# Attention scores of two batches from float32r halves of keys and queries

## Chip, cores and metric

One core of a Trainium2 chip. The metric is the device time of one execution in microseconds (us); a change of 0.5% is about 3.1 us here.

## The reference, cut to what matters

```python
scores = scale * np.matmul(q, k.transpose(0, 1, 3, 2))   # B, H, S, D = 4, 8, 768, 64
scores = np.where(keep, scores + bias, -1e9)             # 8 global keys, 96 local ones
a = softmax(scores)                                      # along the keys
x = np.matmul(a, v)                                      # per head, laid out as (B, S, H * D)
h = np.maximum(x.T @ w_tok1, 0.0) @ w_tok2               # mixes along the sequence
u = x + h.T
out = u + np.maximum(u @ w_ch1, 0.0) @ w_ch2             # mixes along the channels
```

Everything is float32 at the interface; the weights arrive as 64-bit floats.

## The kernel before

Attention goes in 48 units called pairs, numbered v = 0 to 47, twelve to a batch. A pair is two heads (n counts the four pairs of heads) and one strip of 256 queries (j = 0, 1, 2). A strip needs few keys, so its scores are two cuts of 128 queries each: for j = 0 the first cut has 128 keys and the second 256, for j = 1 and 2 both have 256. `load` (L335) brings one tile of 128 rows, which holds keys (columns 0 to 383), queries (384 to 639) and values; rows 0 to 63 belong to the first head, rows 64 to 127 to the second. From batch 1 on these tiles are a ring of four, and a load waits for the values step V of four pairs before.

Each pair then runs through named steps: q (`scale`, L347: the queries times a factor; on GpSimd from batch 1 on, into a tile `qs` of a pool of two buffers), S (`scores`, L374: per cut one unsplit float32 product for each head, the two heads in the two halves of the rows of TensorE), max and exp, sum, inverse and norm, a transpose (through TensorE in early pairs, by DMA from pair 20 on, with `split`, `turn` and `join`), V (`values`, L455, two heads in halves of the columns) and put. The keys are read from the loaded tile `e`, the results go to `sp` in PSUM.

After its twelve pairs a batch goes through `tokens` (L515): transposes N (`xtp`), products J (`pj`) and U (`pu`), which leave u as two float32r parts `uh` and `ul`. Then `channel` (L604) runs 24 rounds k of twelve products F (into `hp`), a ReLU split into `hh` on ScalarE and `hl` on VectorE, and twelve products G (into `acc`). These products are already made of three float32r ones: high by high, high by low, low by high. F of a batch needs u of that batch, and S of a batch from 2 on waits for the last `ul` of the batch before (L486). So scores of batch 2 run among F and G of batch 1, and those of batch 3 among those of batch 2.

The order on every engine comes from a planner (`Plan.record`, L109): a list scheduler with costs in us written beside each step, a rank for each, tokens for buffers (`room`, L240; the one token "q" is held from q to the end of S), and a penalty for a change of the form of TensorE's products ("rows" for S, "columns" for V, none for the others; L155). `InOrder` (L189) keeps each engine's instructions in the order in which the planner recorded them; what an instruction waits for at run time is its data and buffers. All instructions made through it carry line L197, so the rows are told apart by tile names.

Of the kernel before, what the change touches and what calls it, by code (L numbers as in the profile page):

```python
# [8 lines left out]
F32 = mybir.dt.float32  # L9
F32R = mybir.dt.float32r  # L10
# [5 lines left out]
ALU = mybir.AluOpType  # L16
# [4 lines left out]
B, H, S, D = 4, 8, 768, 64  # L21
# [3 lines left out]
P = 128  # L25
NS = S // P
NU = NS // 2
NF = FF // P
# [3 lines left out]
AHEAD = 5  # L32
WIDE = 15
RING = 4
FAR = 20
WARM = 2
PER = H // 2 * NU
# [7 lines left out]
def f32(ap):  # L45
    return ap.bitcast(F32)


class Early:


    def __init__(self, tc, pool, pk, nb):
        nc = tc.nc

        self.slots = [pool.tile([P, 1024], F32, tag=f"e{i}", name=f"e{i}") for i in range(3)]
        self.ni = pool.tile([P, 4], I32, tag="ni", name="ni")
        self.ident = pool.tile([P, P], F32, tag="ident", name="ident")
        self.sc = pool.tile([P, H // 2], F32, tag="sc", name="sc")

        def load(out, in_):  # L60
            tc.stamp_issue_order_token(nc.sync.dma_start(out=out, in_=in_).ins, "loads")

        t = self.slots[2]
        self.warm = t[:, 576:832].bitcast(BF16)
        nc.vector.memset(self.warm, 0.0)
        load(self.slots[0][:, 128:640], pk[0, :, 128:640])
        load(self.ni, nb.broadcast_to([P, 4]))
        load(self.slots[0][:, 640:896], pk[0, :, 640:896])
        load(self.slots[1][:, 128:896], pk[1, :, 128:896])

        def iota(t, base, step, mult):
            nc.gpsimd.iota(t, pattern=[[step, t.shape[-1]]], base=base, channel_multiplier=mult,
                           allow_small_or_imprecise_dtypes=True)

        for h in range(H):
            nc.gpsimd.memset(self.sc[64 * (h % 2):64 * (h % 2) + 64, h // 2:h // 2 + 1], float(2 ** (h + 1)))

        self.rel, self.far, self.glob = t[:, 0:224], t[:, 224:448], t[:, 448:576]
        iota(self.rel, 96, -1, 1)
        iota(self.far, -768, 8, -8)  # L80
        nc.gpsimd.affine_select(out=self.far, in_=self.far, compare_op=ALU.is_ge, fill=-BIG, base=96,
                                pattern=[[-1, 224]], channel_multiplier=1)
        iota(self.glob, 0, 1, 0)
        make_identity(nc, self.ident)


class Plan:
# [13 lines left out]
    def add(self, name, engine, cost, run, after=(), rank=0.0, take=(), give=(), form=None):  # L101

        costs = engine if isinstance(engine, dict) else {engine: cost}
        self.work[name] = dict(name=name, costs=costs, run=run, after=sorted(set(after)), rank=rank, take=take, give=give,
                               form=form, choice=isinstance(engine, dict))
# [98 lines left out]
class Fast:  # L206
# [3 lines left out]
    def __init__(self, ctx, tc, early, pk, nb, w1, w2, wc1, wc2, out):  # L210
        self.tc, self.nc = tc, tc.nc
        nc = tc.nc
        self.pe, self.dve, self.act, self.pool, self.sp = [
            InOrder(tc, e) for e in (nc.tensor, nc.vector, nc.scalar, nc.gpsimd, nc.sync)]
        self.pk, self.nb, self.out = pk, nb, out
        self.pieces = [(x, i) for x in (w1, w2) for i in range(0, 2 * S, 512)]
        self.pieces += [(x, C * f) for f in range(NF) for x in (wc1, wc2)]

        def pool(name, bufs, **kw):
            return ctx.enter_context(tc.tile_pool(name=name, bufs=bufs, **kw))  # L220

        const = self.const = pool("const", 1)

        self.ring = early.slots + [const.tile([P, 1024], F32, tag=f"r{i}", name=f"e{i}") for i in range(RING - 3)]
        self.prep = pool("prep", 2)
        self.soft = pool("soft", 8)
        self.mix = pool("mix", 4)
        self.xs = pool("xs", 8)
        self.us = pool("us", 8)
        self.hl = pool("hl", 6)  # L230
        self.io = pool("io", 3)
        self.wt = pool("wt", 2 * NF)
        self.ps = pool("ps", 1, space=PSUM)
        self.early = early
        self.ident, self.sc = early.ident, early.sc
        self.t, self.x, self.u = {}, {}, {}
        self.W1 = [const.tile([P, NS * TOK], F32R, tag=f"w1{x}", name=f"w1{x}") for x in "hl"]
        self.W2 = [const.tile([P, 2 * S], F32R, tag=f"w2{x}", name=f"w2{x}") for x in "hl"]
        self.A, self.Z = {}, {}
        self.plan = Plan(dict(w=2 * NF, raw=AHEAD, t=3, p=6, mix=4, q=1, x=8, u0=8, u1=8, hl=6), BUSY,  # L240
                         dict(dve=self.dve, act=self.act, pool=self.pool))

    def bank(self, name, *key):
# [91 lines left out]
    def load(self, v):  # L335

        b, n, j = where(v)
        if v < 2:
            t = self.early.slots[v]
        else:  # L340
            t = self.wt.tile([P, 1024], F32, tag="w", name="unit") if b == 0 else self.ring[(v - PER) % RING]
            k0, z = (128, 896) if j == 0 else (0, 1024)
            self.sp.dma_start(out=t[:, k0:z], in_=self.pk[v, :, k0:z])
        vs = [[t[:, o:o + 64] for o in (640 + 128 * e, 704 + 128 * e, 896 + 64 * e)] for e in range(2)]
        self.t[v] = dict(k=t[:, 0:384], q=t[:, 384:640], v=vs)

    def scale(self, v, engine):  # L347

        n = where(v)[1]
        if v < 2:  # L350
            self.load(v)
        t = self.t[v]
        t["qs"] = qs = self.prep.tile([P, 256], F32, tag="qs", name="qs")
        sc = self.sc[:, n:n + 1]
        if engine is self.dve:
            engine.tensor_scalar(out=qs, in0=t["q"], scalar1=sc, scalar2=None, op0=ALU.mult)
        elif engine is self.act:
            engine.activation(out=qs, in_=t["q"], func=AF.Copy, scale=sc)
        else:
            engine.tensor_scalar(out=qs, in0=t["q"], scalar1=sc, scalar2=0.0, op0=ALU.mult, op1=ALU.add)  # L360

    def pair(self, v):

        add = self.plan.add
        dve, act, pool = self.dve, self.act, self.pool
        b, n, j = where(v)
        wide = v < WIDE
        far = v >= FAR

        cuts = ((128, 128, 128), (256, 256, 128)) if j == 0 else ((0, 256, 0), (256, 256, 128))  # L370
        c0 = 1 if j == 0 else 0
        g = {}

        def scores():  # L374
            t = self.t[v]
            g["sp"] = [self.bank("sp", v, e) for e in range(2)]
            for i, (o, w, k0) in enumerate(cuts):
                for e in range(2):
                    r = slice(64 * e, 64 * e + 64)
                    self.pe.matmul(out=g["sp"][e][:, o:o + w], lhsT=t["qs"][r, 128 * i:128 * i + 128],  # L380
                                   rhs=t["k"][r, k0:k0 + w], start=True, stop=True)
# [94 lines left out]
        r = rank("pair", v)  # L476
        if v > 1:
            add(f"load{v}", "sp", 1.4 if j == 0 else 1.85, lambda: self.load(v),
                [f"V{v - RING}"] if v >= PER + RING else [f"V{v - PER}"] if v in (PER, PER + 1) else [], rank("load", v),
                ["w"] if v < PER else [])  # L480
        if v:
            add(f"q{v}", dict(dve=0.3, act=0.4, pool=0.56) if b == 0 else dict(pool=0.56), 0, lambda e: self.scale(v, e),
                [f"load{v}"] if v > 1 else [], r - 8, ["q"])
        wp = ["w"] if wide else ["p", "p"]

        add(f"S{v}", "pe", 0.86 if j else 0.65, scores, ([f"q{v}"] if v else []) + ([f"ul{b - 1}7"] if b > 1 else []), r,  # L486
            [("sp", v, 0), ("sp", v, 1)], ["q"], "rows")
        for e in range(2):
            add(f"max{v}{e}", "dve", 0.7 if j else 0.57, lambda e=e: maxima(e), [f"S{v}"] + ([f"max{v}0"] if e else []),
                r - 10, wp if e == 0 else [], [("sp", v, e)])  # L490
# [202 lines left out]
def where(v):  # L693

    b, r = divmod(v, PER)
    j, n = divmod(r, H // 2)
    return b, n, j
# [5 lines left out]
BUSY = dict(dve=1.9, act=1.4, pool=3.6, sp=2.6)  # L703
# [269 lines left out]
```

## Time and profile before

| what | us |
|---|---|
| median of 3 runs | 629.82 |
| lowest and highest | 627.41, 630.03 |
| the profiled execution | 627.44 |
| its span, first to last instruction | 625.9 |

The span is cut into engines: PE is TensorE's products and PEld its weight loads, DVE VectorE, ACT ScalarE, POOL GpSimd. The profiled execution is at the low end of the three runs; about 1.5 us of it lie outside the span.

### The profile page before, as it was taken

The numbers are of one execution on the slowest core, as the hardware profiler recorded it, in microseconds if no ns is written. First come the engines' busy times: TensorE is split into PE (matmuls) and PEld (weight loads), VectorE is DVE, ScalarE is ACT, GpSimd is POOL, SyncE is SP. The second block draws the span as 40 slices with busy tenths as digits, with TensorE's granted clock in tenths as the row PEclk, the third lists the DMA queues.
The fourth block names the chain that finished last, engine by engine and source line by source line (L and its number), as shares of the span: only waits on it lengthen the run. The fifth ranks groups of instructions, "written<-read, shape, count | busy, mean of one in ns | idle before, by whom it ended". The sixth has DMA issues, their size and how long they took to land.

```text
span 625.9 us, 10504 instructions
## 1 busy us (share of the span) xinstructions
PE 607.2 (97%) x3778; PEld 550.7 (88%) x3778; DVE 354.7 (57%) x922; ACT 258.7 (41%) x712; POOL 201.3 (32%) x312
## 2 busy tenths in 40 slices
PE   5899998999999999999999999999999999999995
PEld 3577896998989999888888999889888999999995
DVE  4999999998733215776663337656765335113112
ACT  5899856763423003565563314545442212111110
POOL 4897755662401001544330114344320024000000
PEclk9999998999999999999999999999999999999998
DMA  6960565333540001576663002565433001001001
GB/s 242 404 230 2 202 234 204 129 109 84 119 84 1 2 0 51 96 174 168 144 129 84 0 1 76 126 148 139 137 56 62 0 1 52 1 0 51 1 0 57
DMA packets 71228, 59.49 MB, mean 95 GB/s; under 512 B 56960, under 2 KB 61184, under 8 KB 71168
## 3 DMA queue, kind: packets, MB, share of 16 engines
q1 hardware_dynamic: 71168, 58.74, 33.5%
q8 instruction: 32, 0.52, 0.3%
q14 instruction: 28, 0.23, 0.1%
HBM read 38.80 MB, written 6.29 MB: 72 GB/s over the span
## 4 chain that ended last, share of the span: by engine, by line
PE 83%; DVE 9%; ACT 3%; POOL 2%; issue 1%; DMA 1%; SPq 0%; DVEq 0%; POOLq 0%; ACTq 0%
PE acc L197 30%; PE hp L197 29%; PE sp L197 7%; PE op L197 6%; DVE t L197 5%; PE pj L197 5%; PE pu L197 4%; ACT pp L197 1%; PE xtp L197 1%; PE tp L197 1%; POOL pp L197 1%; DVE p L197 1%; POOL p L197 1%; DMA e<-pk 1%; DVE x L197 1%
## 5 line engine op out<-in xcount | busy, mean ns | idle before, releaser
L197 PE MATMUL hp<-uh,wc 128*128 128x384 f32 x768 | 210.8, 337 | 0.1
L197 PE MATMUL acc<-hh,wc 128*128 128x384 f32 x768 | 199.6, 341 | 0.0
L197 PEld LDWEIGHTS acc<-hh,wc 128*128 128x128 f32 x768 | 137.1, 189 | 8.3 <-issue 6.7
L197 PEld LDWEIGHTS hp<-uh,wc 128*128 128x128 f32 x768 | 139.9, 188 | 3.1 <-issue 0.8
L197 ACT ACTIVATE hh<-hp 128x384 fp32r<-128x384 f32 x96 | 47.1, 490 | 220.5 <-PE hp L197 201.6
L197 DVE SCALAR_TENSOR_TENSOR hl<-hp,hh 128x384 fp32r<-128x384 f32 x96 | 53.1, 553 | 149.0 <-ACT hh L197 149.0
L197 PE MATMUL acc<-hl,wc 128*128 128x384 f32 x384 | 129.0, 336 | 0.2 <-DVE hl L197 0.2
L197 PE MATMUL hp<-ul,wc 128*128 128x384 f32 x384 | 128.5, 335 | 0.0
L197 POOL TENSOR_SCALAR p<-p,st 128x256 f32<-128x256 f32 (+1 forms) x132 | 82.1, 640 | 44.0 <-ACT p L197 19.6
L197 DVE COPY r<-p 128x1024 uint16<-128x1024 uint16 (+1 forms) x94 | 68.1, 737 | 32.7 <-POOL p L197 17.0
L197 POOL TENSOR_TENSOR ul<-x,uh 128x384 fp32r<-128x384 f32 x24 | 24.6, 1027 | 156.2 <-ACT uh L197 90.0
L197 PEld LDWEIGHTS acc<-hl,wc 128*128 128x128 f32 x384 | 72.3, 188 | 0.5 <-DVE hl L197 0.5
L197 PEld LDWEIGHTS hp<-ul,wc 128*128 128x128 f32 x384 | 72.1, 188 | 0.0
L197 ACT ACTIVATE p<-p,st 128x256 f32<-128x256 f32 (+1 forms) x132 | 63.7, 486 | 18.0 <-DVE st L197 10.9
L197 DVE SCALAR_TENSOR_TENSOR t<-w,t 128x512 int32<-128x512 int32 x60 | 51.9, 865 | 1.1
L197 POOL TENSOR_SCALAR qs<-e,sc 128x256 f32<-128x256 f32 x36 | 21.9, 608 | 90.2 <-DMA e<-pk 53.9
L197 PE MATMUL sp<-e,qs 64*128 64x256 f32 (+1 forms) x304 | 42.0, 396 | 3.9 <-ACT x L197 1.5
L197 PEld LDWEIGHTS sp<-e,qs 64*128 64x128 f32 x304 | 26.2, 195 | 13.4 <-issue 6.8
L197 POOL TENSOR_SCALAR pp<-pp,st 128x256 f32<-128x256 f32 (+1 forms) x60 | 34.9, 597 | 8.0 <-DVE st L197 5.7
L197 DVE TENSOR_TENSOR pl<-xtp,ph 128x512 fp32r<-128x512 f32 x24 | 15.5, 686 | 25.6 <-ACT ph L197 25.6
L197 PE MATMUL op<-r,e 128*64 128x128 f32 (+1 forms) x304 | 29.7, 321 | 0.0
L197 POOL TENSOR_TENSOR wc<-t,wc 128x512 fp32r<-128x512 f32 x16 | 22.7, 1419 | 19.5 <-ACT wc L197 18.2
(89 smaller groups left out, 742.1 us busy)
## 6 DMA issues: line engine op xcount, KB each, us to landing
w<-wc SPq DMA_DIRECT2D x24, 512.0 KB, 5.2
e<-pk SPq DMA_DIRECT2D x24, 512.0 KB, 3.6
out<-o SPq DMA_DIRECT2D x32, 192.0 KB, 1.9
e<-pk SPq DMA_DIRECT2D x13, 384.0 KB, 3.7
unit<-pk SPq DMA_DIRECT2D x8, 512.0 KB, 9.0
w<-w SPq DMA_DIRECT2D x6, 512.0 KB, 9.4
p<-r SPq DMA_TRANSPOSE x56, 3.2
unit<-pk SPq DMA_DIRECT2D x2, 384.0 KB, 3.7
```

What stands on the lines that cost most here:

```text
L197: ins = getattr(self.engine, name)(*args, **kw)
```

## The change

For pairs from number 24 on (batches 2 and 3) q now writes its result over the queries in the loaded tile. A new step qh on ScalarE copies keys and queries (640 columns, or 512 for j = 0) to a float32r tile, a new step ql on VectorE or GpSimd, whichever the planner finds free, subtracts that from the original to give the low part. Both parts lie in a pool with one buffer, under a new token "qk" that is held from qh to the end of S; the token "q" is given back after ql. S makes each product as three float32r ones (high by high, high queries by low keys, low queries by high keys), the two heads next to each other in the order, and its planned cost changes.

```diff
+PARTS = 24
+        self.parts = pool("parts", 1)
-        self.plan = Plan(dict(w=2 * NF, raw=AHEAD, t=3, p=6, mix=4, q=1, x=8, u0=8, u1=8, hl=6), BUSY,
+        self.plan = Plan(dict(w=2 * NF, raw=AHEAD, t=3, p=6, mix=4, q=1, qk=1, x=8, u0=8, u1=8, hl=6), BUSY,
-        self.t[v] = dict(k=t[:, 0:384], q=t[:, 384:640], v=vs)
+        self.t[v] = dict(t=t, k=t[:, 0:384], q=t[:, 384:640], v=vs)
-        t["qs"] = qs = self.prep.tile([P, 256], F32, tag="qs", name="qs")
+        qs = t["qs"] = t["q"] if v >= PARTS else self.prep.tile([P, 256], F32, tag="qs", name="qs")
+        def high():
+
+            z = 128 * c0
+            t = self.t[v]["t"][:, z:640]
+            g["qk"] = [self.parts.tile([P, 640], F32R, tag=x, name="qk")[:, z:] for x in "hl"]
+            act.copy(out=g["qk"][0], in_=t)
+
+        def low(engine):
+            h, l = g["qk"]
+            engine.tensor_tensor(out=l, in0=self.t[v]["t"][:, 128 * c0:640], in1=f32(h), op=ALU.subtract)
+
         def scores():
             t = self.t[v]
             g["sp"] = [self.bank("sp", v, e) for e in range(2)]
+            if v >= PARTS:
+                z = 128 * c0
+                for i, (o, w, k0) in enumerate(cuts):
+                    for n, (x, y) in enumerate(((0, 0), (0, 1), (1, 0))):
+                        for e in range(2):
+                            r, q = slice(64 * e, 64 * e + 64), 384 - z + 128 * i
+                            self.pe.matmul(out=g["sp"][e][:, o:o + w], lhsT=g["qk"][x][r, q:q + 128],
+                                           rhs=g["qk"][y][r, k0 - z:k0 - z + w], start=n == 0, stop=n == 2)
+                return
+        ready = f"q{v}"
+        if v >= PARTS:
+            add(f"qh{v}", "act", 0.63 if j else 0.52, high, [f"q{v}"], r - 8, ["qk"])
+            add(f"ql{v}", dict(dve=0.76 if j else 0.62, pool=1.7 if j else 1.35), 0, low, [f"qh{v}"], r - 8, (), ["q"])
+            ready = f"ql{v}"
-        add(f"S{v}", "pe", 0.86 if j else 0.65, scores, ([f"q{v}"] if v else []) + ([f"ul{b - 1}7"] if b > 1 else []), r,
-            [("sp", v, 0), ("sp", v, 1)], ["q"], "rows")
+        add(f"S{v}", "pe", ((0.7 if j else 0.53) if v >= PARTS else 0.86 if j else 0.65), scores, ([ready] if v else []) + ([f"ul{b - 1}7"] if b > 1 else []), r,
+            [("sp", v, 0), ("sp", v, 1)], ["qk"] if v >= PARTS else ["q"], "rows")
```

## Rows read from the trace of the kernel before

**Rows 1.** The page's busy time of each engine, share of the span, instructions.
```profile
PE 607.2 (97%) x3778; PEld 550.7 (88%) x3778; DVE 354.7 (57%) x922; ACT 258.7 (41%) x712; POOL 201.3 (32%) x312
```

**Rows 2.** Busy time by stretch: engines in turn, granted clock, DMA share, GB/s.
```profile
150.00:247.00 97.00, 97.00 (x580) 91.89 (x579) 41.52 (x92) 26.77 (x63) 13.94 (x20) 1.00 0.21 50
247.00:320.00 73.00, 72.96 (x472) 61.96 (x472) 49.18 (x161) 40.28 (x119) 28.41 (x50) 1.00 0.65 140
320.00:382.00 62.00, 62.00 (x370) 58.47 (x368) 27.59 (x54) 20.00 (x45) 12.96 (x17) 1.00 0.19 49
382.00:464.00 82.00, 82.00 (x545) 73.19 (x544) 53.20 (x167) 37.60 (x119) 30.00 (x50) 1.00 0.52 119
464.00:520.00 56.00, 56.00 (x329) 53.08 (x330) 23.66 (x47) 14.30 (x35) 9.85 (x13) 1.00 0.10 20
```

**Rows 3.** The chain that ended last, 235 to 520 us: start, us, what, count.
```profile
by line: PE acc L197 37.9%; PE hp L197 32.3%; PE op L197 8.2%; PE sp L197 8.1%; PE pu L197 5.8%; PE pj L197 5.8%; PE xtp L197 1.8%; issue 0.0%
...
250.94 0.86 PE sp L197 x8
...
264.56 2.08 PE hp L197 x12
...
271.60 2.29 PE hp L197 x12
273.89 1.06 PE sp L197 x8
...
317.44 1.93 PE sp L197 x16
...
336.84 1.75 PE xtp L197 x16
...
339.63 5.49 PE pj L197 x24
...
375.00 6.24 PE hp L197 x36
...
382.28 1.51 PE sp L197 x16
...
498.51 8.32 PE pu L197 x48
```

**Rows 4.** Groups by form, 240 to 480 us: busy us, mean ns, idle before.
```profile
L197 PE MATMUL sp<-e,qs 64*128 64x256 f32 x160 | 22.5, 395 | 0.0
...
L197 POOL TENSOR_SCALAR qs<-e,sc 128x256 f32<-128x256 f32 x22 | 12.7, 579 | 72.7 <-DMA e<-pk 48.0 <-DVE st L197 7.8 <-issue 6.3
...
L197 POOL TENSOR_TENSOR ul<-x,uh 128x384 fp32r<-128x384 f32 x8 | 8.1, 1019 | 46.7 <-ACT uh L197 30.5 <-DVE o L197 16.1
...
L197 ACT CAST uh<-x 128x384 fp32r<-128x384 f32 x10 | 5.1, 513 | 8.4 <-DVE o L197 4.6 <-DVE x L197 3.8
...
L197 PE MATMUL sp<-e,qs 64*128 64x128 f32 x32 | 3.8, 310 | 0.0
...
L197 ACT CAST ph<-xtp 128x512 fp32r<-128x512 f32 x6 | 3.2, 588 | 7.4 <-PE xtp L197 5.5 <-PE pj L197 1.9
...
L197 DVE TENSOR_TENSOR ul<-x,uh 128x384 fp32r<-128x384 f32 x3 | 1.7, 554 | 0.2
```

**Rows 5.** Timeline of the weight loads, 247.5 to 248.3 us (pair 24).
```profile
247.62 0.60 PEld L197 LDWEIGHTS sp<-e,qs 64*128 64x128 f32 x8 [0.25 <-issue]
```

**Rows 6.** Timeline of GpSimd, 262 to 277 us: start, us, [idle before and releaser].
```profile
266.13 0.48 POOL L197 TENSOR_SCALAR qs<-e,sc 128x256 f32<-128x256 f32 x1 [1.31 <-DMA e<-pk]
271.39 0.48 POOL L197 TENSOR_SCALAR qs<-e,sc 128x256 f32<-128x256 f32 x1 [4.78 <-DMA e<-pk]
```

**Rows 7.** Timeline of TensorE, 262 to 277 us (pairs 28 and 29).
```profile
267.38 1.13 PE L197 MATMUL sp<-e,qs 64*128 64x256 f32 x8
...
273.82 1.13 PE L197 MATMUL sp<-e,qs 64*128 64x256 f32 x8
```

**Rows 8.** Busy time of hp's instructions: PE, PEld, DVE, ACT, clock, DMA.
```profile
519.15:626.00 106.85, 53.45 (x288) 50.05 (x288) 13.36 (x24) 11.81 (x24) 0.98 0.07 24
```

## The prediction

> **What bounds the kernel now.** I read the page's busy times first: TensorE has work in 97% of the span, the next engine, VectorE, in 57% [rows 1]. A busy TensorE can still hide waits, so the stretches come next. From 150 to 520 us, which takes in everything that the change touches, TensorE is busy in all but 0.04 us, at full granted clock (1.00, the 2.4 GHz level), while VectorE is busy in 53.2 of 82.0 us in the densest stretch, ScalarE in 37.6 and GpSimd in 30.0 [rows 2]. The chain that ended last says the same: between 235 and 520 us it is products from end to end, 8.1% of them scores, and the time put down to waiting is nil [rows 3]. So here a product that gets shorter brings the end forward by what it gives up, and work on the other engines costs nothing until a product waits for it.
>
> **Products of a pair with 256 keys.** There are 16 such pairs among the 24 (j = 1 and 2). The float32 product is two loads and two passes of products for each head (160 rows of 256 columns and 32 of 128 [rows 4] are 192, eight for each of 24 pairs). Eight in a row for a single pair take 1.06 us on the chain, sixteen for two pairs 1.93 [rows 3]: a further pair costs 0.87 us, four steps of 0.217, since both heads run side by side. In the new form it is six steps of 256 columns. No such product is in the trace, but float32r products of the full array are: 36 of 384 columns take 6.24 us, 0.173 each, and 24 of 512 columns 5.49 us, 0.229 each [rows 3]. The line through both gives 0.117 for 256 columns (0.173 less 0.056). Six steps are 0.70 us, so 0.17 less than 0.87, and 16 pairs give **-2.7 us**. Bounds: a step cannot be below 0.109, the pace of sixteen float32 transposes (1.75 us [rows 3]) that also load 128 columns each time, so -3.4 us; and if the fixed part of a float32r step came on top of the full float32 pace of 0.109 (0.013 more, what 0.173 has above 384 columns at 2.4 GHz), 0.122 a step and -2.2 us.
>
> **Products of a pair with j = 0.** There are 8. Two such pairs take 1.51 us and one 0.86 [rows 3], so one costs 0.65. New: three steps of 256 columns at 0.117, and three of 128. The line would give 0.062 for these, but each brings a load of 128 columns, and the transposes show that a load and a product of this length come no closer than 0.109. I take 0.109: 0.68 in all, 0.03 more than before, **+0.2 us** for 8. Lower bound: the line, -0.9 us. Upper bound: a product of 128 columns in float32r no faster than the unsplit one, which needs two steps of 0.109: +2.9 us. The nearest rows are the loads, so I stay at the 0.109.
>
> What speaks against the change here is a rule of the Trainium skill ("TensorE: Matmul & The Clock Gate", section "LDWEIGHTS (loading the stationary operand)"): a load's time goes by its columns, P / 1.2 ns, and not by its rows, so half the rows save nothing; 128 columns are 107 ns by it, as an estimate. By that the j = 0 pairs come out at no gain, as they do from the transposes, where a count of columns streamed would give 8 x 0.17 = 1.4 us. The trace agrees in the loads' pace (0.109).
>
> **Side by side.** The eight loads of pair 24 all lie within 0.60 us [rows 5]. One after another at 0.109 they would take 0.87, so the two halves load at the same time, and the steps above hold for both heads.
>
> **Changes of form.** Twelve F products take 2.08 us after their like and 2.29 after a score or value step; a score step alone takes 1.06 where its marginal price is 0.87 [rows 3]. So each change of form costs 0.2 us. Before, four score steps stand doubled on the chain (two of each kind; one of each in [rows 3]). With one buffer for the parts, the copy of the next pair begins only when S of this pair is done, and copy plus subtraction take over 1.5 us (next paragraph), so doubles cannot stay without a wait. Taken apart, each costs two more changes, 0.4 us, together 1.6 us; where a value step stands between the two scores it costs nothing. Bounds 0 and +1.6. The order is made anew by the planner; I take **+0.6 us**.
>
> **The split.** Removed: nothing but a buffer; q has the same instruction and place on GpSimd. Added: 24 copies on ScalarE. 384 columns take 513 ns and 512 take 588 [rows 4], so 640 take some 0.66 us; 16 x 0.66 + 8 x 0.59 = 15 us. 24 subtractions: 384 columns take 0.554 us on VectorE and 1.019 on GpSimd [rows 4], by the columns 0.92 or 1.70 for 640 and 0.74 or 1.36 for 512; 21 us on VectorE or 38 on GpSimd. Their cover is the idle time: in 247 to 320 and 382 to 464 us VectorE has 52.6 us free of 155, ScalarE 77.1, GpSimd 96.6 [rows 2]. Without that cover the time is not theirs in full, but what S then waits. Where S waits: q, copy and subtraction are now a chain of 0.66 + 0.92 = 1.6 us (2.4 with GpSimd) longer before it. q itself is often late, as GpSimd spends 48.0 us waiting for loads of `e` [rows 4]. For pair 28 q ends at 266.61 and S starts at 267.38; for pair 29 it is 271.87 and 273.82 [rows 6, 7]. With the longer chain, pair 28 is ready 0.8 to 1.6 us after that place, pair 29 at most 0.5 us after it. The planner knows nearly the same length (0.63 + 0.76) and will put other products ahead, of which F and G give two us at a time; it does not know of queues on ScalarE and VectorE. Behind a copy that waits for S stand exp of an older pair and the ReLU of `hp`, for which the next G waits. Bounds 0 and the whole lateness of these two pairs, 2.1 us; I take **+0.7 us**.
>
> **Attention as a whole** gets later by some 2 us for each turn of the ring, three turns a batch, so about 6 us. Tokens of batch 3 end their products at 506.8 (498.51 + 8.32) [rows 3], but the 288 F products of its channel part start only at 519.15 [rows 8]: 12 us of the work of batch 2 are left to fill in. Nothing.
>
> **Sum.** -2.7 + 0.2 + 0.6 + 0.7 = -1.2 us against the profiled execution's 627.44 (span 625.9 and 1.5 around it), so 626.2. That execution is 2.4 us below the median of the three runs; against the median of 629.82 it is **628.6 us**.
>
> **Rivals.**
> 1. *More of the gain is kept.* Steps at 0.109, no double lost, no wait: -3.4 us and nothing else, 626.4. For it: no product waited between 150 and 520 us before, in spite of chains as long. Against: the float32r rows of 384 and 512 columns stand above a pure stream.
> 2. *S becomes a wait (slower).* The subtraction is late at the place that the planner gave S, as ScalarE's and VectorE's queues are in order. The price: if the four doubled scores stay doubled and each waits 1.6 to 2.4 us, that is 6.4 to 9.6, with pairs 28 and 29 up to 11.7; less the 2.5 of the products, +4 to +9 us, 634 to 639. It decides from waits of 2.5 us in total on, and is slower by over 0.5% from 5.6. Against: 0.04 us of idle TensorE in rows 2.
> 3. *A half's next load is not hidden behind its own product (slower).* Then a step is 0.109 + 0.117 for 256 columns, 0.109 + 0.062 for 128. A pair takes 1.36 instead of 0.87 (16 x 0.49) or 1.19 instead of 0.65 (8 x 0.54): +12 us, 642. Against it: for full rows a load is hidden in the F rows (0.173 a step), and in halves the old step of 0.217 has no room for 0.109 on top of 256 columns in two passes. The Trainium skill has such a rule (same page, "Part 3: Packing small matmuls"): a load overlaps a product in flight only where the row group differs. Rows 3 speak against it.
> 4. *Attention ends too late.* If the longer chain moves the tokens of a batch by more than the 12 us, TensorE idles for the rest: at twice the 6 us, nothing; at three times, +5 net, 635.
>
> **How the numbers follow.** My sum, with its terms within their bounds, has 0.72; rival 1 has 0.12, rival 2 0.09, rival 3 0.04, rival 4 0.03. About 0.5%, 3.1 us, is what a measurement of this kernel can tell from no change. With every term at its bound my sum runs from -3.4 - 0.9 = -4.3 to -2.2 + 2.9 + 1.6 + 2.1 = +4.4 us; the terms are seldom all good or all bad, so its own range is 626 to 631.5. Most of it is within 0.5%; of rival 1 some two thirds are beyond it, with a chance or two from an order that also saves changes of form: faster 0.11. Rivals 2 to 4 and the upper corner of the sum are slower: 0.17. The rest, 0.72, is no difference. The range that leaves out 2 in 10 is 625 to 633.
>
> **What would show it.** After: twelve products a pair in `sp`, the pace of two steps of one head 0.117 for 256 columns and 0.109 for 128; S alone on the chain 0.9 us for either kind; no score steps doubled without an idle TensorE ahead of the second; TensorE busy without gaps from 247 to 480 us; copies of 0.66 us on ScalarE. The prediction is wrong if TensorE shows idle time released by the new subtraction, if the steps are above 0.13, or if 128 columns take 0.2.

## The result and the profile after

The changed kernel takes 631.91 us (median; 630.66 to 634.13) against 629.07 for the kernel before in the same measurement: ratio 1.0052, interval 1.0037 to 1.0066. The time lies in the range that was given, but it is slower where a slight gain was forecast.

The page's busy times of the changed kernel, and its chain that ended last, 240 to 530 us (the view cuts this line off at its end):

```profile
PE 611.0 (97%) x3874; PEld 555.8 (88%) x3874; DVE 370.8 (59%) x929; ACT 269.2 (43%) x732; POOL 235.6 (37%) x333
...
by line: PE acc L198 28.7%; PE hp L198 26.5%; PE pu L198 5.7%; PE op L198 5.7%; PE pj L198 5.7%; PE sp L198 5.3%; DVE r L198 4.9%; POOL p L198 3.2%; DMA p<-r 2.9%; DVE p L198 2.1%; issue 2.1%; PE xtp L198 1.8%; DMA out<-o 1.6%; ACT p L198 1
```

Against [rows 1] GpSimd has 34 us more. The chain is no longer products from end to end, as it was in [rows 3]: the copy `r` on VectorE, GpSimd's norm `p` and DMA are on it.

The profiled execution (633.99 us, span 631.9) is among the slowest of its kernel and the one before was among the fastest, so their spans overstate the difference. What the change can touch is read more exactly from a stretch between two products: from the last G product of batch 0, just ahead of the first G of batch 1, to the first F of batch 3. Timelines of TensorE, the kernel before, then the changed one (start, us):

```profile
240.07 0.34 PE L197 MATMUL acc<-hl,wc 128*128 128x384 f32 x1
...
519.15 0.33 PE L197 MATMUL hp<-uh,wc 128*128 128x384 f32 x1
```

```profile
242.21 0.33 PE L198 MATMUL acc<-hl,wc 128*128 128x384 f32 x1
...
526.27 0.33 PE L198 MATMUL hp<-uh,wc 128*128 128x384 f32 x1
```

The stretch took 279.1 us and takes 284.1: +5.0. (2.1 us of the longer span lie ahead of it, where the granted clock was 0.96 on average between 60 and 150 us, for 0.98 in the kernel before.) I use this stretch for all kernels below, and split it in three: the products of S, the changes of form at 0.2 us each (counted in the order of the trace: 73 before, 81 after), and waits, which are the rest. So "waits" is a remainder against the kernel before, not a sum of waits seen.

The products did what was forecast. Chain of the changed kernel, pieces with scores:

```profile
321.16 0.91 PE sp L198 x12
...
386.88 0.89 PE sp L198 x12
```

A pair with 256 keys in both cuts takes 0.91 for 1.06, a pair with j = 0 0.89 for 0.86 [rows 3]: 16 x -0.15 + 8 x 0.03 = -2.2 us. So 5.0 = -2.3 (as e4 below measures it) + 8 x 0.2 + 5.7 of waits. TensorE's weight loads name who was late (240 to 490 us: total, times, longest):

```profile
PEld op L198 <- DVE r L198: 2.7, 4, 1.4
PEld sp L198 <- DVE hl L198: 1.6, 1, 1.6
PEld op L198 <- DVE st L198: 1.5, 3, 1.0
```

These are mostly value steps `op` that wait for VectorE's copy `r`, and one S that waits for `hl`. No line of this view names the parts `qk`: no product was seen to wait for the subtraction itself. The first of them in the timeline, 260.7 to 264.2 us (GpSimd, VectorE, TensorE):

```profile
260.71 1.28 POOL L198 TENSOR_TENSOR qk<-e,qk 128x512 fp32r<-128x512 f32 x1
260.78 1.64 DVE L198 COPY r<-p 128x768 uint16<-128x768 uint16 x1 [0.29 <-POOL p L198]
...
262.46 0.65 PE L198 MATMUL op<-r,e 128*64 128x256 f32 x2
...
263.44 0.59 DVE L198 COPY r<-p 128x768 uint16<-128x768 uint16 x1
...
264.09 0.43 PE L198 MATMUL op<-r,e 128*64 128x256 f32 x2 [0.98 <-DVE r L198]
```

The copy of 16-bit words, 768 columns wide, takes 0.59 us when alone (263.44). The one that starts 0.07 us after a subtraction on GpSimd takes 1.64: it ends at 262.42, 0.43 after the subtraction (261.99). All that VectorE has behind it is late by 1.0 us, the next such copy among it, and V waits for that one. The planner gave GpSimd 21 of the 23 subtractions between 240 and 490 us, and eleven copies there take over 1.1 us (none did before). The two groups by form, 240 to 490 us:

```profile
L198 POOL TENSOR_TENSOR qk<-e,qk 128x640 fp32r<-128x640 f32 x14 | 22.8, 1628 | 31.7 <-ACT qk L198 31.7
L198 DVE COPY r<-p 128x768 uint16<-128x768 uint16 x27 | 21.6, 810 | 8.0 <-POOL p L198 5.0 <-DMA p<-r 2.9
```

The mean copy of this form took 623 ns in the kernel before, by the same view.

The Trainium skill describes this ("SBUF — State Buffer", section "Who interferes with whom"): VectorE in its two-port modes, which copies can enter, and GpSimd share a pair of ports, whoever comes first has it for its whole instruction, and the other is blocked and not slowed. The trace agrees, in both directions. The twelve copies that start while GpSimd subtracts end 0.42 to 0.47 us after it with 768 columns and 0.55 to 0.70 with 1024, a little less than such a copy takes alone (medians of 0.56 and 0.75). The two subtractions that start 0.10 and 0.18 us into a copy take 2.01 and 1.97 us, the other twelve of 640 columns 1.55 to 1.58:

```profile
439.33 2.01 POOL L198 TENSOR_TENSOR qk<-e,qk 128x640 fp32r<-128x640 f32 x1 [0.36 <-ACT qk L198]
```

### The profile page after: what moved, and what is told of

Its sections match the earlier page's. It is cut to its first block, busy times and chain, and to the rows that moved or that the text cites. A ratio compares the mean times of both kernels' runs of the same rounds, so it can differ in the third digit from the quotient of the medians.

```text
span 631.9 us, 10707 instructions
## 1 busy us (share of the span) xinstructions
PE 611.0 (97%) x3874; PEld 555.8 (88%) x3874; DVE 370.8 (59%) x929; ACT 269.2 (43%) x732; POOL 235.6 (37%) x333
## 4 chain that ended last, share of the span: by engine, by line
PE 74%; DVE 12%; POOL 4%; ACT 4%; DMA 3%; issue 2%; SPq 0%; DVEq 0%; POOLq 0%; ACTq 0%
PE hp L198 26%; PE acc L198 26%; PE sp L198 5%; PE pj L198 5%; DVE t L198 5%; PE op L198 5%; PE pu L198 4%; POOL p L198 2%; DVE r L198 2%; DVE p L198 2%; ACT pp L198 1%; PE xtp L198 1%; PE tp L198 1%; DMA p<-r 1%; POOL pp L198 1%
## 5 line engine op out<-in xcount | busy, mean ns | idle before, releaser
L198 DVE COPY r<-p 128x1024 uint16<-128x1024 uint16 (+1 forms) x98 | 82.5, 850 | 37.6 <-DMA p<-r 19.0
L198 POOL TENSOR_TENSOR qk<-e,qk 128x640 fp32r<-128x640 f32 (+1 forms) x21 | 31.9, 1517 | 47.9 <-ACT qk L198 47.9
L198 PE MATMUL op<-r,e 128*64 128x128 f32 (+1 forms) x304 | 31.8, 322 | 1.9 <-DVE r L198 1.3
L198 PEld LDWEIGHTS op<-r,e 128*64 128x64 f32 x304 | 19.6, 136 | 14.3 <-issue 5.2
L198 DVE TENSOR_TENSOR pl<-xtp,ph 128x512 fp32r<-128x512 f32 x24 | 15.4, 685 | 24.3 <-ACT ph L198 24.3
L198 ACT ACTIVATE pp<-pp,st 128x256 f32<-128x256 f32 (+1 forms) x60 | 28.5, 487 | 1.3 <-DVE st L198 1.3
```

The lines of the kernel that those rows point to most:

```text
L198: ins = getattr(self.engine, name)(*args, **kw)
```

## The experiments

Ratios are to the kernel before on the same chip, with the 95% interval. "Waits" is the stretch less 279.1, less the change in products (-2.3; -2.5 where j = 0 is not split; 0 unsplit), less 0.2 for each change of form above 73.

| kernel | stretch, us | start to end | changes of form | waits | ratio |
|---|---|---|---|---|---|
| before | 279.1 | 240.07 to 519.15 | 73 | 0 | 1 |
| changed | 284.1 | 242.21 to 526.27 | 81 | 5.7 | 1.0052 (1.0037 to 1.0066) |
| e13 its order alone | 282.3 | 241.72 to 524.00 | 81 | 1.6 | 1.0010 (0.9996 to 1.0023) |
| e14 order, products | 278.6 | 241.44 to 520.03 | 81 | 0.2 | 0.9965 (0.9952 to 0.9979) |
| e15 and ScalarE's copies | 278.7 | 239.63 to 518.30 | 81 | 0.3 | 0.9953 (0.9939 to 0.9968) |
| e1 and subtractions on VectorE | 282.0 | 239.54 to 521.54 | 81 | 3.6 | 1.0017 (1.0004 to 1.0029) |
| e12 short GpSimd instruction | 279.6 | 241.62 to 521.22 | 81 | 1.2 | 0.9988 (0.9973 to 1.0003) |
| e3 split work, unsplit products | 285.3 | 239.49 to 524.77 | 81 | 4.6 | 1.0070 (1.0050 to 1.0090) |
| e4 products, own order | 276.4 | 239.79 to 516.19 | 71 | 0 | 0.9967 (0.9953 to 0.9982) |
| e9 seven hl | 285.6 | 239.44 to 525.06 | 81 | 7.2 | 1.0050 (1.0031 to 1.0068) |
| e10 e1 and seven hl | 282.7 | 238.11 to 520.83 | 81 | 4.3 | 1.0025 (1.0011 to 1.0039) |
| e2 planned for VectorE | 279.1 | 241.15 to 520.25 | 80 | 0.9 | 0.9983 (0.9969 to 0.9997) |
| e11 e2 and seven hl | 279.0 | 241.04 to 520.00 | 80 | 0.8 | 0.9961 (0.9948 to 0.9974) |
| e5 e2 without j = 0 | 281.1 | 240.63 to 521.77 | 78 | 3.6 | 0.9998 (0.9982 to 1.0015) |
| e6 e2, two buffers | 281.3 | 241.09 to 522.36 | 74 | 4.3 | 1.0017 (1.0002 to 1.0033) |
| e7 e6 without j = 0 | 281.2 | 239.56 to 520.73 | 74 | 4.4 | 1.0013 (0.9996 to 1.0030) |
| e8 two buffers | 281.3 | 241.41 to 522.71 | 76 | 3.9 | 1.0000 (0.9983 to 1.0016) |

The stretch comes from one execution of each kernel, and that of the kernel before is the zero of the whole column. Against it the runs put nearly every kernel lower: the ratio, times the 628 us or so of the kernel before, gives 1.1 to 2.6 us less than the difference of the stretches for all but e4 (0.6 more) and e9 (3.4 less). So what is counted from the kernel before, the 5.7 us of waits above among it, may be too high by about that much. Differences between two changed kernels hold in both measures: from e15 to e1 3.3 us by the stretches and 4.0 by the ratios, from e15 to the changed kernel 5.4 and 6.2.

**e1, the subtraction on VectorE in the same order.** Theory A was GpSimd's hold on VectorE's copies; theory B the new order.

```diff
             h, l = g["qk"]
-            engine.tensor_tensor(out=l, in0=self.t[v]["t"][:, 128 * c0:640], in1=f32(h), op=ALU.subtract)
+            dve.tensor_tensor(out=l, in0=self.t[v]["t"][:, 128 * c0:640], in1=f32(h), op=ALU.subtract)
```

> The stretch from the first G product of batch 1 to the first F product of batch 3 took 279.1 us before and 284.1 after. Here the order on TensorE is that of the changed kernel; only the subtractions that GpSimd did are issued on VectorE. Theory A (a subtraction on GpSimd holds up VectorE's 16-bit copies that run beside it, so value steps V come late): no such copy above 1.1 us, the three waits of V (together 2.7 us) gone, the stretch near 281, the whole about level with the kernel before (ratio 0.998 to 1.002). Theory B (the new order itself, with its 81 changes of form for 73 and its longer chain before S, costs the time whoever subtracts): the stretch stays at 283.5 to 284.5, ratio 1.004 to 1.007.

By form, 240 to 490 us, this kernel:

```profile
L198 DVE COPY r<-p 128x768 uint16<-128x768 uint16 x27 | 16.4, 619 | 7.4 <-POOL p L198 4.8 <-DMA p<-r 2.5
L198 DVE TENSOR_TENSOR qk<-e,qk 128x640 fp32r<-128x640 f32 x16 | 13.2, 825 | 2.9 <-ACT qk L198 2.4
```

No copy above 1.1 us is left, and 2.1 us came back. Not 3: waits of 3.6 us stayed, so A is right and not the whole.

**e13, e14, e15, the same order with its parts put back one by one.** First the planned order with the products of before and nothing for qh and ql:

```diff
         def high():
...
-            act.copy(out=g["qk"][0], in_=t)
+            pass
...
         def low(engine):
...
-            engine.tensor_tensor(out=l, in0=self.t[v]["t"][:, 128 * c0:640], in1=f32(h), op=ALU.subtract)
+            pass
...
         def scores():
...
+                        self.pe.matmul(out=g["sp"][e][:, o:o + w], lhsT=t["qs"][r, 128 * i:128 * i + 128],
+                                       rhs=t["k"][r, k0:k0 + w], start=True, stop=True)
```

> The changed kernel's planned order with the unsplit products of before and without any copy or subtraction (the two steps are in the plan and issue nothing). If the order alone costs only its eight more changes of form: stretch 280.4 to 281.2 (279.1 + 1.6), ratio 1.001 to 1.004. Rival: the 3.6 us of waits that are left with the subtraction on VectorE lie in the order itself; 283 to 285, ratio 1.006 or more.

282.3: 1.6 of changes of form and 1.6 of waits, between the two answers. The order by itself costs 3.2 us by the stretch; by the runs it is only 0.6 (-0.3 to 1.4), which fits the first answer, so its size is not settled. Then the three products, with parts made once for pair 24 (later scores are those of pair 24, so the output is not the reference's):

```diff
+            if v == PARTS:
+                self.once = [self.parts.tile([P, 640], F32R, tag=x, name="qk") for x in "hl"]
...
+            g["qk"] = [x[:, z:] for x in self.once]
```

> The changed kernel's order and its three products, with the parts made once for pair 24 and used by all later pairs (their scores are those of pair 24; the output is not the reference's), so no copies and subtractions after the first. If the order costs only its changes of form: stretch 278 to 278.8 (279.1 - 2.3 + 1.6), ratio 0.997 to 1.000. Rival, waits in the order itself: 280.5 to 282.5.

278.6 as expected (the ratio lies just below its range): the shorter products give back 3.7 (2.8 by the ratios), more than their own 2.3. TensorE's weight loads wait 0.2 us for `r` here and 1.3 in e13; that this is because the order was planned for shorter products is not shown. One wait of S for `hl` stays, 0.8 us, so the 0.2 of the table does not mean that there is none. Then ScalarE's copy for each pair, with low parts of zero:

```diff
             act.copy(out=g["qk"][0], in_=t)
...
-            engine.tensor_tensor(out=l, in0=self.t[v]["t"][:, 128 * c0:640], in1=f32(h), op=ALU.subtract)
+            g["qk"] = [h, self.once[:, 128 * c0:]]
```

> The changed kernel's order, products and ScalarE copies for each pair, but no subtraction after the first (the low parts are zero, which leaves the correction by low parts out). With the subtraction on VectorE the stretch was 282.0, with a shorter GpSimd instruction in its place 279.6. If the subtraction is the loss, wherever it stands: 278.2 to 279.5. If the copies on ScalarE and their wait for S of the pair before cost as well: 280 to 281.5.

278.7: the copies and S's wait for them cost nothing (0.1 us). The longest wait of TensorE's weight loads in e15, and the same view of e1:

```profile
PEld sp L198 <- DVE hl L198: 0.9, 1, 0.9
```

```profile
PEld op L198 <- DVE r L198: 1.6, 4, 0.6
PEld acc L198 <- DVE hl L198: 1.3, 2, 1.1
PEld sp L198 <- DVE hl L198: 1.0, 1, 1.0
```

From e15 to e1 the one thing added is the subtraction of each pair, on VectorE, with S after it: +3.3 us. From e15 to the changed kernel it is the same with 21 of them on GpSimd: +5.4. So the subtraction is the loss, wherever it stands, and GpSimd is the worse place.

Why VectorE is late with `hl` for G in e1 (1.3 us above, nothing in e15) is in its timeline, 304 to 307 us, with the product that waited:

```profile
305.00 0.82 DVE L198 TENSOR_TENSOR qk<-e,qk 128x640 fp32r<-128x640 f32 x1
305.73 0.74 DVE L198 COPY r<-p 128x1024 uint16<-128x1024 uint16 x1
306.37 0.54 DVE L198 SCALAR_TENSOR_TENSOR hl<-hp,hh 128x384 fp32r<-128x384 f32 x1
306.96 0.44 PE L198 MATMUL acc<-hl,wc 128*128 128x384 f32 x1 [0.82 <-DVE hl L198]
```

The later wait of S for `hl` is in its chain, 300 to 312 us:

```profile
303.55 4.54 DMA e<-pk
...
308.12 0.48 POOL p L198
...
308.63 0.18 DVE r L198
...
309.52 0.55 DVE hl L198
...
310.11 0.98 PE sp L198 x10
```

The subtraction stands 0.82 us ahead of `r`, on which the DMA transpose waits, and of `hl`, for which G waits 0.82. In the chain a load comes first, then a norm on GpSimd, the copy `r` and `hl`, whose end frees the bank for S. Each is an engine in order, and a late start is handed on. But e15 has that wait of S too (0.9 for 1.0 us), without any subtraction, so it belongs to the order and is not part of the 3.3.

**e12, a shorter instruction on GpSimd.** I took two inputs from the same memory for what holds VectorE.

```diff
+            if engine is pool:
+                engine.tensor_scalar(out=l, in0=self.t[v]["t"][:, 128 * c0:640], scalar1=0.0, scalar2=0.0, op0=ALU.mult,
+                                     op1=ALU.add)
+                return
```

> The changed kernel's order; in the pairs whose subtraction GpSimd did, it instead multiplies the columns by zero, one input and not two (the low parts of these pairs are zero, which leaves the correction by low parts out). If two inputs from the same memory are what holds VectorE's copies: no copy of 16-bit words above 1.1 us, stretch near 282 as with the subtraction on VectorE, ratio 1.000 to 1.003. Rival, any long GpSimd instruction holds them: copies of 1.2 us and more remain, stretch 283.5 to 284.5.

279.6, better than either answer: 4.5 us below the changed kernel. But not for the reason given. By form, 240 to 490 us, and the timeline at 294 us:

```profile
L198 POOL TENSOR_SCALAR qk<-e 128x640 fp32r<-128x640 f32 x14 | 10.4, 745 | 24.4 <-PE sp L198 23.0 <-issue 1.2
```

```profile
294.62 0.72 POOL L198 TENSOR_SCALAR qk<-e 128x640 fp32r<-128x640 f32 x1
294.68 1.21 DVE L198 COPY r<-p 128x1024 uint16<-128x1024 uint16 x1
```

The copy beside it still ends 0.55 us after it, as beside a subtraction. One input holds VectorE as two do; it is over in 0.745 us on average where the subtraction takes 1.628. It also waits for no copy of ScalarE, so the chain ahead of S is shorter; no run tells the two apart.

**e3, the split work with unsplit products.** Does S's own wait for the parts matter?

```diff
             if v >= PARTS:
...
+                        self.pe.matmul(out=g["sp"][e][:, o:o + w], lhsT=t["qs"][r, 128 * i:128 * i + 128],
+                                       rhs=t["k"][r, k0:k0 + w], start=True, stop=True)
                 return
```

> Order, copies and subtractions of the changed kernel, but S makes the unsplit float32 products of before from the scaled queries and the keys, so it waits for no subtraction. The products of the 24 pairs are then 2.1 us longer than in the changed kernel (16 x 0.15 less 8 x 0.03). Theory A: the long copies beside GpSimd stay, the waits of V stay (about 2.7 us), the stretch is 285 to 286.5, ratio to the kernel before 1.006 to 1.011. If instead S's wait for the parts were the loss, V and S would wait no more and the stretch would be 281 to 282, ratio near 1.004.

285.3, as theory A said: S needs no parts here, nine copies still take over 1.1 us, and 4.6 us of waits stay.

**e4, the products with the work left out, in an order of their own.** qh and ql leave the plan; one step fills the parts for pair 24, and as in e14 the output is not the reference's.

```diff
-            add(f"qh{v}", "act", 0.63 if j else 0.52, high, [f"q{v}"], r - 8, ["qk"])
-            add(f"ql{v}", dict(dve=0.76 if j else 0.62, pool=1.7 if j else 1.35), 0, low, [f"qh{v}"], r - 8, (), ["q"])
+            if v == PARTS:
+                add("once", "act", 2.0, once, [f"q{v}"], r - 8)
```

> Copy and subtraction are made once, for pair 24, and every later pair uses these parts for its three products (its scores are those of pair 24, so the output is not the reference's): the shorter products without the work of splitting. Theory A: no long copies, no waits of V or S, the products alone count: stretch 276.5 to 278 (279.1 less 2.1, give or take some changes of form), ratio 0.995 to 0.998. Theory B: a new order with the lower cost of S loses it again: stretch 279 or more, ratio 1.000 or above.

276.4, a tenth below theory A's range, with 71 changes of form and no single wait of a weight load above 0.5 us: the products alone are worth 2.7 less 0.4, so 2.3 us, if the rest is as in the kernel before. By the runs all of it is 2.1 us.

**e9 and e10, a seventh buffer for hh and hl.** In the changed kernel's chain at 300 to 316 us a store stands ahead of the ReLU:

```profile
302.37 2.81 POOL p L198 x3
305.18 0.02 issue
305.20 0.69 DVE r L198
305.89 0.48 DVE o L198
306.37 0.02 issue
306.39 0.57 DVE o L198
306.96 0.19 SPq L198
...
307.82 4.76 DMA out<-o
312.59 0.02 issue
312.61 0.50 ACT hh L198
```

The reading was that a buffer that the store holds is what `hh` lacks.

```diff
-        self.hl = pool("hl", 6)
+        self.hl = pool("hl", 7)
```

> The changed kernel, its planned order kept, with one more buffer in the pool of hh and hl (seven where the planner counts six). In the changed kernel TensorE waits at 307 to 313 us because a ReLU on ScalarE has no free buffer until a store has landed, which GpSimd's norms, a copy on VectorE and a load on the DMA queue held up in turn. If that chain is the reason: the wait of 1.75 us inside S and the two of 0.3 before it go, stretch 281.5 to 283, ratio 1.001 to 1.004. Rival: the buffers are not what it waits for; the stretch stays at 283.5 to 284.5.

> The changed kernel's order, subtractions on VectorE and seven buffers for hh and hl. If the two causes account for the waits, 282.0 less the 2.1 at that place gives a stretch of 279.5 to 280.5, and what is left above the 276.8 of shorter products is 1.6 for eight more changes of form and 1 to 2 of small waits; ratio 0.998 to 1.000. Rival: waits move elsewhere in the order; 281.5 or more.

Both missed: 285.6 for 284.1 and 282.7 for 282.0. In e9 `hh` still waits for a store to land (2.4 us for 2.7), so the seventh buffer did not take this wait away, and whether a buffer free in time would have helped is not shown. Some 1.6 us of e9's stretch is the clock: 11 steps after 311.7 us take 0.15 more each, and the granted clock falls to a mean of 0.54, near its lower level, behind 1.4 us without products:

```profile
300.00:311.00 11.00, 9.45 (x63) 7.58 (x63) 8.67 (x22) 4.66 (x16) 7.38 (x10) 1.00 0.72 180
311.70:315.20 3.50, 3.50 (x14) 3.45 (x12) 3.37 (x13) 2.70 (x9) 1.56 (x1) 0.54 0.97 167
316.00:330.00 14.00, 14.00 (x107) 12.60 (x105) 9.74 (x27) 6.49 (x21) 9.43 (x12) 1.00 0.48 103
```

The changed kernel has a gap of the same length at 312 us, and its clock stays at 1.00.

**e2 and e11, planned for VectorE alone**, e11 with seven buffers in plan and pool:

```diff
-            add(f"ql{v}", dict(dve=0.76 if j else 0.62, pool=1.7 if j else 1.35), 0, low, [f"qh{v}"], r - 8, (), ["q"])
+            add(f"ql{v}", dict(dve=0.76 if j else 0.62), 0, low, [f"qh{v}"], r - 8, (), ["q"])
```

> The planner is told that only VectorE can subtract, so the order is made anew. Theory A: no long copies, no wait of V above 0.5 us, stretch 279 to 281.5, ratio 0.996 to 1.002. Theory B: some new order with more changes of form than 73 and waits at S; stretch 283 or more, ratio above 1.003.

> Subtractions planned for VectorE alone, seven buffers of hh and hl in the pool and in the plan. The order is new again; with the scatter that new orders showed (279.1 to 281.3), 278 to 281; if the buffers are worth what they are in the fixed order, 278 to 279 and a ratio of 0.995 to 0.998. Rival: waits as in other new orders; 280 to 281.5, ratio 1.000 to 1.002.

279.1 and 279.0, waits of 0.9 and 0.8: the order planned with the subtraction on VectorE alone has few waits. e11 at 0.9961 is the best kernel here that computes the whole reference, 0.4% faster than the kernel before by the runs, though its stretch is no shorter.

**e5 to e8, fewer pairs and two buffers.** e5 to e7 keep the subtraction on VectorE. e5 splits only pairs with j above 0; e6 and e8 give the parts two buffers (low parts in the weights' idle ones); e7 is both.

```diff
-        self.parts = pool("parts", 1)
+        self.parts = pool("parts", 2)
...
-            g["qk"] = [self.parts.tile([P, 640], F32R, tag=x, name="qk")[:, z:] for x in "hl"]
+            g["qk"] = [p.tile([P, 640], F32R, tag=x, name="qk")[:, z:] for p, x in ((self.parts, "h"), (self.io, "io"))]
```

> Subtraction on VectorE alone, and only the 16 pairs with two cuts of 256 keys are split; the 8 pairs with j = 0 keep their unsplit products. The stretch was 279.1 with all 24 split (VectorE alone). If the j = 0 pairs lose by being split (0.76 to 0.79 us of products, plus their copies and subtractions): 278 to 278.8, of which 0.3 from products and 0.4 from two fewer changes of form; ratio to before 0.996 to 0.999. Rival: the order decides and the split of j = 0 is free; 279 to 280.5.

> Subtraction on VectorE alone, two buffers for the parts (the low part lies in the buffers of the weights' stage, idle by then). TensorE's order has 6 changes of form fewer than with one buffer. If the single buffer cost what the changes of form cost (0.2 us each): stretch 277.5 to 278.3, ratio 0.994 to 0.998. Rival: what is left after moving the subtraction is the wait for hl near the end of the first half of batch 1's channel part, which buffers of the parts don't touch; 279 to 279.5, ratio near 0.998.

> Both of the former together. If their gains add: stretch 277 to 278, ratio 0.993 to 0.997, the best of all that split in place. Rival: a wait elsewhere takes it; 278.5 or more.

> Two buffers for the parts, the planner's choice between GpSimd and VectorE kept. The theory that GpSimd's subtractions are the larger loss: VectorE's copies of 1.2 to 2.1 us beside them stay, waits of V stay, stretch 282.5 to 284 (284.1 less 1.0 for five fewer changes of form), ratio 1.002 to 1.006. Rival, the single buffer is the larger loss: 279 to 281, ratio 1.000 or below.

The first answers all missed, e5 to e7 too high, e8 too low: 281.1 to 281.3. e7 lies within its rival's answer (278.5 or more), e8 just above its rival's (279 to 281). In e8's new order GpSimd has only 8 of the 24 subtractions, so it tells little of GpSimd's share. Two buffers did take out changes of form (74 to 76 are left), but each new order came with its own waits of 3.6 to 4.4 us. A sum of terms from one order doesn't carry to another.

## Why the prediction was wrong

- **What bounds the kernel**: right. Between 240 and 520 us each delay of a product shows in full in the stretch.
- **Products**: right. -2.5 us forecast, -2.3 measured (e4); 0.91 and 0.89 for a pair were named. The loads are hidden and both heads run side by side, so rival 3 didn't happen; steps at 0.109, as in rival 1, didn't either (0.118 in the middle of the changed kernel's steps of 256 columns).
- **Changes of form**: the price of 0.2 was right, the number not: eight more, 1.6 us, the upper bound, where +0.6 was taken. In the changed kernel no score steps stand doubled.
- **The split**, the step that failed: "Their cover is the idle time", and then only S was priced as a waiter, at +0.7 with a bound of 2.1. The waits are 5.7 us by the stretch. Idle time of VectorE is no cover when what stands behind the subtraction in its queue, `r` and `hl`, has a due time: 3.3 us come from that alone (e15 to e1). With GpSimd, whose instruction also stops VectorE's copies, it is 5.4 (e15 to changed). The bound left out that a second engine is held up, and looked at the subtraction's own reader. It named what stands behind the copy on ScalarE, not what stands behind the subtraction on VectorE. The planner does know of these queues (`Plan.record` keeps for each engine when it is free); what no cost in it says is that a subtraction on GpSimd lengthens VectorE's copies. ScalarE's copy takes 0.73 us and not 0.66, but was costed as free, and is (e15).
- **Rival 2** had the sign and not the mechanism: S doesn't wait for the subtraction (e3 keeps most of the waits without any such wait, and no weight load of the changed kernel waits for `qk`); V and G and S wait for other work of VectorE. Its price of +4 to +9 fits the stretch's +5.0, by luck, and not the runs' +2.8.
- **Rival 4**: TensorE had no gap before the first F of batch 3; tokens of batch 3 end 15.4 us later (522.3 for 506.8), far more than the 6 forecast, which leaves 4.0 us of the slack of 12.
- The sum: -2.3 + 1.6 + 5.7 = +5.0 in the profiled stretch; the runs' median moved by 2.8. The profiled executions differ by 6.5: 5.0 in the stretch, 2.1 ahead of it, 0.5 outside the span, and 1.1 less behind the last product (5.6 us for 6.7). Nearly all kernels have that gap between stretch and runs, so it is more than scatter of the one changed execution; whether the kernel before had a short stretch in its one execution, or the rest of the program got shorter, is not shown.

Left open: how much the order alone costs (3.2 us by the stretch of e13, 0.6 by its runs) and which of the engines' queues hands on its waits, and why the orders of e5 to e8 wait 3 us more than those of e2 and e11. The planner's costs are another suspect that no run tested: it has 0.63 us for a copy that takes 0.73, and 0.76 for a subtraction on VectorE that takes 0.825.

## What to carry to other kernels

Work on an engine with idle time is free only if nothing with a due time stands behind it in that engine's queue, and on GpSimd only if VectorE has no copies at that time: read what follows it in order, not the busy share. Where a planner orders the work, keep its order and change one thing at a time to find a cause, since each new order brings waits of its own, here up to 4.4 us, as large as the gain that was sought. Tell the planner the place that is best on the chip, and then time a few orders. Check a difference of stretches against the runs as well: one execution of the kernel before is the zero of every such difference.

## What was not expected of the hardware

- A copy of 16-bit words on VectorE that starts while GpSimd is at work ends 0.41 to 0.75 us after GpSimd's instruction, with one input or two, no later than a copy alone would take (medians of 0.56 with 768 columns, 0.75 with 1024): 1.64 us beside 1.28, 1.21 beside 0.72. The other way round, a subtraction of 640 columns on GpSimd that starts 0.10 us into a copy takes 2.01 us for 1.55 to 1.58.
- On GpSimd a subtraction of two tiles of 640 columns takes 1.628 us on average, a product by a constant 0.745; on VectorE the subtraction takes 0.825, less than the 0.92 that its columns gave.
- TensorE's granted clock fell to a mean of 0.54 for 3.5 us behind 1.4 us without products in one execution (e9), which cost some 1.6 us more; in the changed kernel the same gap left it at 1.00.
